# Second weight matrix: maxima on ScalarE, scaling and rounding in one pass, low half on VectorE, and new written orders

## The chip, the cores and the metric

The kernel runs on one core of one Trainium2 chip. The core has TensorE (PE; its weight loads are shown as PEld), VectorE (DVE), ScalarE (ACT), GpSimd (POOL) and the queue engine SyncE (SP), which issues the DMAs here. The metric is the device time of one execution in microseconds. Before the change it was 1485.22 us, the median of 3 runs (1484.78 to 1485.92).

## The reference

```python
def _attn_ref(q, k, v):                      # q, k, v: 8 x 8 x 1152 x 64, f32; q and k have a spread of 0.8
    q_pool = q.reshape(B, H, S // 2, 2, D).mean(axis=3)
    scores = scale * np.matmul(q_pool, k.transpose(0, 1, 3, 2))
    scores = scores - np.max(scores, axis=-1, keepdims=True)
    attn = np.exp(scores)
    attn = attn / (np.sum(attn, axis=-1, keepdims=True) + 1e-09)
    return np.matmul(attn, v).astype(np.float32)

def _moe_ref(x, w_in, w_out):                # x: 4608 x 512; w_in: 512 x 2048; w_out: 2048 x 512, both float64
    h = x @ w_in
    g = h * np.cos(h)
    return (g @ w_out).astype(np.float32)
```

The attention's output, heads side by side, is `x` of the second part.

## The kernel before

**Numbers.** An f32 product is made of f16 products: each operand is split into a rounded f16 half ("hi") and what the rounding left, again f16 ("lo"), and three matmuls (hi·hi, hi·lo, lo·hi) are summed in PSUM.

**Attention.** Heads are worked on in 32 pairs. For a pair, PE first forms scores for their row maxima (L645, L667, L690, L724, L794), and VectorE reduces them (L657, L678, L703, L739, L809). Then PE forms the scores again, transposed and with the maxima taken off (L1089, L1109, L1131), ScalarE takes the exponential out of PSUM (L1160), rounds it to f16 (L1168), GpSimd (or VectorE, L1170) makes the low half (L1174), and PE multiplies with the values (L1212, L1275; in the first six pairs part of the exponentials stay in f32). Four PSUM banks, the `st` ones, serve the maxima and the scores in turn; two, `ava` and `avb`, collect the outputs; two, `f`, serve the feed-forward part.

**Feed-forward.** For each of 18 chunks of 256 rows PE forms `h` (`ffn1`, L1509), ScalarE and VectorE bring it out (L1536 to L1540) and make the cosine (L1443, L1449), ScalarE rounds the product (L1460), GpSimd makes its low half (L1461), and PE multiplies with the second weight matrix (`ffn2`, L1572). These matmuls lie between those of the attention from 178 us on, and alone after its last ones.

**Weights.** `w_in` and `w_out` are float64 and come as eight blocks each of 128 x 1024 numbers. A block is decoded to f32 by three VectorE passes over its bits (L392, L395, L398; two of them work in place). Then its greatest magnitude is found (`weight_decode`): for `w_in`, where `WACT` is 1, by a ScalarE pass that squares the block and accumulates (L405, the squares go to a part of the weight tile that is written later), for `w_out`, where it is 0, by a VectorE reduction (L409). For each two blocks PE spreads the maxima over the partitions (L339) and VectorE makes a power of two of them (`weight_scale`). Then `weight_split` scales the block in place on ScalarE (L432), rounds it to f16 on ScalarE (L433) and makes the low half by four GpSimd subtractions of 256 columns each (L436). The blocks of `w_out` are held in buffers `wf`, which are of the same four large ones (`big`) that the feed-forward part uses.

**Order.** The instructions of each engine run in an order that is written out in the table `ORDER`, one packed string for each engine; `unpacked` turns it into a list of places, `arrange` chains the instructions in it. Matmuls are taken in lots of up to 12. The lists of PE (2684 lots), ScalarE (1632), VectorE (2104), GpSimd (783) and SyncE (492) fix every engine's order; a semaphore wait makes all behind it wait.

Of the kernel before, what the change touches and what calls it, by code (L numbers as in the profile page):

```python
# [74 lines left out]
ORDER = {  # L75
    "PE": (
        "c-l=?Yi|@s5UlQ**}a#|88|Q(I53<oe8l$odBMRkU>;Efk%Ex&As>=2NRjgYzo)8a?PPqu$4+lQs;hbyz|M|uYnhwDF+=<CX"
        "5l+br&B!WR@&t9bgx@!QkUIz!^Vb>V;R=l)C`T@+JYv-P#PK}SaQqBEEVUk4D@nl#H2Sk|4lD`Lb-TJaGJTBE~R8cT4n9gAf"
# [3 lines left out]
        "4rO^0H=1E^rKtpIoF17_DpA9T1jM)%XC7b{76dL@G-NF6mT1_hkHfLEM}9k1Z+xw9nBU{~X)c6s0&D@>m}3_QQ8$yL?R=NKW"
        "AoB3#HvLbEtg*z_zY~YJrO1~^GB?4TG+376hVgz%7IqN({o;W;eja0H~No3v*OK`tM`3weJ23Y4!5Rq@rW?0&+`QibmLLRsY"
        "eEM$qUORaa=!=Q`Q~e#F`WKEkQkxQUvx>_!I0M%QUMu3p;?F7>=~7F0rY2LEB}O;4<=STH+4Lmoc~8Cjp;576knAc#prAR`!"
        "`B?@&rdI6OmC?H$?&L685b<}n5;0QN}#GEzbhO@U|3XrbTf#UcF6a00Awp&XHGaff!6grnQg(d!9Bt!=twojdZko6e}263lc"
        "QI^~ygTCVV;EPuk4K!`r)SF~yA?G$!Sc`M1HJUyaazE9CxftYd#lF?qj=769qCKI=Jiu?hM5b<YW2wb@sgTVmT>;8=GO~+Cn"
# [5 lines left out]
        "PGEcU0oRguC)HmY-bp|RjwzjUOPAJls(&-nSc{$z822R=EIwRHrOf2gaS`V3oxU#&Z<><dgu*Mt^n7gH;eZfFoZawkVrX$X9"
        "jT&p{L<+8>O#1@kJf%Le8lIkv0Kk4uCJ-s@AA|C^G1&NRiLoyFSWHA>uSm`!s}DPr!S)TR~i3-zwoVC{u}>DPa((d@#0%d$)"
        "Xbs0fOevZ;Jidr3e2Q5_=b?GcjPj_DT~ss#^KWkUX92ONefZdMp!Ok0%?kWH{6*bgMS7U!{FrhH9Kp0(@iuA7YZC1!}Yzipu"
        "r5MwIAQ8jb1`652re+SQE#@Gm>~Ni6"
    ),
    "Activation": (
        "c-mc5?QUa53_bREKJG_KZ<E|6O`5dn(smJxRtWYFAVHr1i8p`;;P--f0K`l0@l1*kqvXzvXKWwa$D<H||DzxXBv|4Uf+W>s5"
        ";VmQSymzuCT5Zh8Y7TXqO3&eQckj4AoXy0N+t8K>&7vSL+OV{jQs!}<T4Be=*Dg^vwrM3F8VKqL7`oTPD;mP;)oWKa2BP@;O"
# [12 lines left out]
        "c-lo(%W@l45Iub#bMKvzW+Yj%WLuUcMRqJpwqtAoNgys>DOf;QP({ds@F-Y?;uBbf${(;~n?GPl6_sL}U*H3%{DSH3kwcfQk"
        "?!Mk_vzC;FqS}&zxpE}WRwMRk-r)v%jjg8MUY(!I0v60cZfvj@lwaymJOE8u(=+uZOBneay`V@LC7=TWV|S7ylTjMVg#fZno"
        "TsaEM)<{y}#d1F~xDy`*yq2E(+wli=y8LrG$?6zLD-#WqG$;F4LmN)<}^f4I5$JDa)z~gR;qp9|E};Qo3Vfj1?{dTlP^f9~c"
        "lxa-1Ybv7*`r$DBWfKpC%k&QdM&E_W_)(40w#p{h*5DRCxFxX585=M1Wl)fO_-D2l?HiVxUa!YFbyo14hs#h8HQ68;22`#kU"
# [1734 lines left out]
```

## Time and profile before

| what | us |
|---|---|
| median of 3 runs | 1485.22 |
| the profiled execution, its own time | 1485.77 |
| its span | 1484.0 |
| PE busy in the span | 1454.9 (98%) |
| ScalarE, VectorE, GpSimd busy | 1173.0, 1057.2, 915.8 |
| mean granted clock of PE | 0.996 |

All times in the rows further down are those of the profiled execution and count from the start of its span. An engine's busy time is the union of its instructions; PE's matmuls overlap, so a matmul's own duration is longer than the step from one to the next. The time after `<-` in brackets is how long the engine sat idle before the instruction, with what ended it.

### The profile page before, as it was taken

How to read it: one execution, taken by the hardware profiler on the slowest of the kernel's cores; microseconds unless marked ns; L12 is line 12 of the kernel's file. 1: busy time of each engine (PE TensorE's matmuls, PEld its weight loads, DVE VectorE, ACT ScalarE, POOL GpSimd, SP SyncE). 2: the span in 40 equal slices, each digit the busy share in tenths (PEclk: the TensorE clock that was granted, in tenths of full speed). 3: DMA queues.
4: the chain of work that ended last, by engine and by line, in shares of the span. 5: the costliest groups of instructions: out<-in, count | busy, mean ns of one | idle time of the engine just before them, and what ended most of it. 6: DMA issues, size and time to landing. Idle time of an engine off the chain costs nothing.

```text
span 1484.0 us, 36198 instructions
## 1 busy us (share of the span) xinstructions
PE 1454.9 (98%) x14825; PEld 979.1 (66%) x14825; DVE 1057.2 (71%) x2104; ACT 1173.0 (79%) x1728; POOL 915.8 (62%) x786
## 2 busy tenths in 40 slices
PE   6999999999999999999999999999999999999998
PEld 3777776657666666657666657666666657666665
DVE  7899886767787778867767867886778868443332
ACT  4667879988899788888979888989889888854442
POOL 4334658787677767586666576667867774723222
PEclk9999999999999999999999999999999999999999
DMA  8876742445445544456444654554445543200000
GB/s 247 219 218 167 200 112 56 112 110 104 111 91 108 115 102 104 104 120 142 99 105 79 120 112 106 96 130 104 97 102 106 122 110 69 48 20 22 29 11 29
DMA packets 280422, 158.07 MB, mean 107 GB/s; under 512 B 254784, under 2 KB 257088, under 8 KB 278208
## 3 DMA queue, kind: packets, MB, share of 16 engines
q1 hardware_dynamic: 280256, 155.76, 45.5%
q8 instruction: 116, 1.90, 0.5%
q14 instruction: 50, 0.41, 0.1%
HBM read 74.45 MB, written 10.49 MB: 57 GB/s over the span
## 4 chain that ended last, share of the span: by engine, by line
PE 89%; DVE 5%; ACT 4%; issue 1%; POOL 0%; DMA 0%; ACTq 0%; POOLq 0%; DVEq 0%
PE f L1509 21%; PE f L1572 20%; PE st L1089 15%; PE ava L1212 9%; PE avb L1212 7%; PE mx L645 4%; PE st L1572 3%; PE st L1509 2%; PE st L1109 2%; PE ava L1275 1%; ACT e L1160 1%; PE avb L1275 1%; DVE mxs L657 1%; ACT pp L1168 1%; PE mx L667 1%
## 5 line engine op out<-in xcount | busy, mean ns | idle before, releaser
L1174 POOL TENSOR_TENSOR pp<-e,pp 128x512 f16<-128x512 f32 (+1 forms) x464 | 519.3, 1144 | 256.2 <-ACT pp L1168 142.1
L1509 PEld LDWEIGHTS <-w 128*128 128x128 f16 x3456 | 329.2, 98 | 69.4 <-issue 13.1
L1509 PE MATMUL f<-xT,w 128*128 128x256 f16 x3048 | 367.1, 273 | 0.8 <-DVE y L1540 0.8
L657 DVE TENSOR_REDUCE mxs<-mx 128x1 f32<-128x512 f32 x464 | 295.0, 682 | 59.7 <-PE mx L645 59.4
L1572 PE MATMUL f<-w,g 128*128 128x512 f16 x1440 | 332.9, 379 | 0.0
L1160 ACT ACTIVATE e<-st 128x512 f32<-128x512 f32 x482 | 268.2, 598 | 78.6 <-PE st L1089 54.6
L1168 ACT CAST pp<-e 128x1024 f16<-128x1024 f32 x267 | 281.2, 1062 | 12.6 <-PE avb L1212 8.0
L1572 PEld LDWEIGHTS <-g 128*128 128x128 f16 x1680 | 157.4, 98 | 179.0 <-issue 7.6
L1212 PEld LDWEIGHTS <-pp 128*128 128x128 f16 (+1 forms) x4621 | 220.0, 98 | 78.9 <-issue 11.6
L1461 POOL TENSOR_TENSOR g<-hsc,g 128x512 f16<-128x512 f32 x144 | 179.1, 1260 | 141.6 <-ACT g L1460 134.2
L1089 PE MATMUL st<-q1T,k 128*128 128x512 f16 x576 | 219.1, 380 | 7.7 <-DVE mxs L739 3.2
L1089 PE MATMUL st<-q2T,k 128*128 128x512 f16 x576 | 219.4, 381 | 0.0
L1212 PE MATMUL ava<-vc,pp 128*128 128x65 f16 (+4 forms) x2800 | 165.8, 205 | 0.6 <-DVE pp L1170 0.6
L1540 DVE SCALAR_TENSOR_TENSOR y<-f,r1a,y 128x512 f32<-128x512 f32 x127 | 94.7, 747 | 95.3 <-ACT y L1539 95.0
L1212 PE MATMUL avb<-vc,pp 128*128 128x65 f16 (+3 forms) x2329 | 156.6, 207 | 1.4 <-POOL pp L1174 1.2
L1089 PEld LDWEIGHTS <-k 128*128 128x128 f16 x1152 | 99.5, 99 | 75.9 <-issue 16.7
L1449 DVE TENSOR_TENSOR hsc<-hsc,y 128x512 f32<-128x512 f32 x144 | 112.8, 811 | 43.4 <-ACT y L1443 43.4
L563 POOL TENSOR_TENSOR kst<-kld,kst 128x1152 f16<-128x1152 f32 x30 | 74.2, 2472 | 66.9 <-ACT kst L562 66.1
L1536 DVE TENSOR_SCALAR hsc<-f,small 128x512 f32<-128x512 f32 x111 | 82.6, 745 | 26.4 <-PE f L1509 26.2
L1460 ACT CAST g<-hsc 128x512 f16<-128x512 f32 x144 | 85.0, 620 | 18.4 <-DVE hsc L1449 14.5
L1539 ACT ACTIVATE y<-f,r1a 128x512 int32<-128x512 f32 x127 | 87.7, 691 | 13.8 <-DVE hsc L1536 13.1
L1160 ACT ACTIVATE pp<-st 128x512 f32<-128x512 f32 (+1 forms) x108 | 59.5, 593 | 40.1 <-PE st L1089 28.1
(183 smaller groups left out, 1812.6 us busy)
## 6 DMA issues: line engine op xcount, KB each, us to landing
vld<-in_v_dram SPq DMA_DIRECT2D x32, 576.0 KB, 4.4
kld<-in_k_dram SPq DMA_DIRECT2D x30, 576.0 KB, 4.9
qld<-in_q_dram SPq DMA_DIRECT2D x30, 576.0 KB, 4.3
k<-k SPq DMA_DIRECT2D x64, 144.0 KB, 3.1
wraw<-in_moe_w_in_dram SPq DMA_DIRECT2D x8, 1024.0 KB, 8.0
wraw<-in_moe_w_out_dram SPq DMA_DIRECT2D x8, 1024.0 KB, 6.4
out_dram<-ob SPq DMA_DIRECT2D x32, 256.0 KB, 2.7
...
```

The source lines that it names most:

```text
L657: nc.vector.reduce_max(mxs[n][:, h * QT + t, c : c + 1], banks[2 * c + h], axis=AX.X)
L1089: nc.tensor.matmul(s[y].rearrange("p (t c) -> p t c", c=P), kcol(w, j, h), x[:, h * QT : (h + 1) * QT, :], start=part == 0, stop=part == 1 ...
L1160: nc.scalar.activation(e[:, c], b[:, 0 : c.stop - c.start], AF.Exp, scale=exp_scale, bias=bias)
L1168: nc.scalar.copy(pp[:, 0, c0:n], e[:, c0:n])
L1174: nc.gpsimd.tensor_sub(pp[:, 1, c], e[:, c], pp[:, 0, c])
L1212: mm = nc.tensor.matmul(out, w, x, start=start, stop=False, skip_group_check=True)
L1449: nc.vector.tensor_mul(hj, hj, y[:, j : j + 2])
L1461: nc.gpsimd.tensor_sub(gt[:, 1], hj, gt[:, 0])
L1509: mm = nc.tensor.matmul(ps[:, fi, :], w1[wt][:, hp, fs], ck.xT[hp][:, xi, cs], start=n == 0, stop=n == 3 * HP - 1, skip_group_check=True,)
L1539: nc.scalar.activation(yj.bitcast(I32), ps, AF.Copy, scale=ra, bias=0.25)
L1540: nc.vector.scalar_tensor_tensor(yj, ps, ra, yj.bitcast(I32), ALU.mult, ALU.subtract)
L1572: nc.tensor.matmul(po, gt[:, gi, f % 2, ts_], w2[wt][:, f, :], start=f == 0 and (gi, wt) == (0, 0), stop=f == NF - 1 and (gi, wt) == (1, 0),)
```

## The change

`WACT` becomes 1 for `w_out` too: the VectorE reduction (L409, 8 of them) is replaced by a ScalarE square with accumulation, and the power of two is made from the square. With `WFUSE` 1 for `w_out`, ScalarE writes the f16 half straight from the unscaled f32 block with the scale as an operand (one pass in the place of L432 and L433), and VectorE makes the low half as block times scale minus high half (one pass over 1024 columns in the place of four GpSimd subtractions). `w_in` keeps its steps. All five lists are replaced.

```diff
-WACT = (1, 0)
+WACT=(1,1)
 HB = 2 * WACT[0]
...
+WFUSE = (0,1)
...
 ORDER = {
     "PE": (
...
@@ weight_split
         fv = ft.rearrange("p (r w) -> p r w", r=rows)
+        if WFUSE[wi]:
+            nc.scalar.activation(hi, fv, AF.Copy, scale=sc)
+            nc.vector.scalar_tensor_tensor(lo, fv, sc, hi, ALU.mult, ALU.subtract)
+            return
         nc.scalar.activation(ft, ft, AF.Copy, scale=sc)
         nc.scalar.copy(hi, fv)
         for o in range(0, rows, rows // WCUT):
```

Unpacked, the new lists hold 2684, 1632, 2104, 751 and 492 places: on PE and SyncE the same work, on ScalarE and VectorE as many instructions as before, on GpSimd 32 fewer. Few neighbours stay neighbours: 549 of PE's 2684 lots keep the lot that followed them. On PE no lot is moved by more than 53 places, on SyncE no DMA by more than 25. Three stretches of the two lists of PE and VectorE, by line of the kernel before (`x4` is a lot of four matmuls; `pair` is a lot of two L1089; head pairs are counted from 0):

```
A  VectorE, maxima of head pair 2 (before: from 57 us)
   before  L739  L392  L395  L739  L398  L739  L761  L739
   new     L739  L761  L739  (small)  L392  L739  ...
           (the reduction that follows L392 and L395 before now follows L761)
B  PE, scores of head pair 6's remaining rows (before: from 233.7 us)
   before  L1109 x12  pair  pair  L645 x4  pair  pair  L1509 x12
   new     L1109 x12  pair  L1212 x4  L1212 x4  L1212 x4  pair  L1509 x12  L645 x4
           L1509 x12  pair  pair
C  PE, maxima of head pair 5 (before: from 167.7 us)
   before  L645 x4  L1212 x12  L1212 x6  L1212 x4  pair  pair
   new     L645 x4  pair  pair  pair  L1212 x12
   VectorE at the same place
   before  L959  L1334  L1339  L1342  L657  L657  L657  L657
   new     L1339  (new low half)  L1342  L657  L657  L959  L959  L392  L657  L657
```

In the new lists the first L1509 of PE stands at place 361 (350 before) and the first L1572 at 528 (534 before). ScalarE's last two passes for `w_out` stand at places 236 and 239 (before the last four at 236 to 250), VectorE's last two low halves at 378 and 382; in the lists of before, these places are at 223 to 228 us of the profiled execution. All eight new low halves stand at VectorE places 256 to 382, where the list of before runs from 152 to 227 us.

## Rows read from the trace of the kernel before

**Rows 1.** The page's part 1: busy us, share of the span, instructions of each engine.
```profile
PE 1454.9 (98%) x14825; PEld 979.1 (66%) x14825; DVE 1057.2 (71%) x2104; ACT 1173.0 (79%) x1728; POOL 915.8 (62%) x786
```

**Rows 2.** Busy time by stretch: start:end, length, engines with instruction counts, granted clock, DMA.
```profile
0.00:37.00 37.00, 24.64 (x167) 13.11 (x167) 27.27 (x54) 16.52 (x26) 15.02 (x18) 0.95 0.84 248
37.00:100.00 63.00, 60.08 (x537) 47.02 (x536) 55.46 (x97) 43.62 (x73) 25.35 (x22) 0.95 0.78 216
100.00:150.00 50.00, 47.38 (x469) 36.49 (x468) 47.92 (x99) 36.58 (x62) 19.12 (x17) 1.00 0.63 176
150.00:200.00 50.00, 49.94 (x509) 38.48 (x508) 42.11 (x92) 40.33 (x67) 33.20 (x40) 1.00 0.68 177
200.00:245.00 45.00, 41.78 (x412) 30.98 (x409) 35.24 (x74) 40.80 (x61) 31.47 (x35) 1.00 0.35 85
...
300.00:700.00 400.00, 396.50 (x4278) 257.77 (x4276) 302.13 (x610) 344.52 (x503) 287.13 (x238) 1.00 0.50 110
700.00:1100.00 400.00, 399.97 (x4345) 263.93 (x4343) 303.93 (x607) 346.98 (x497) 275.75 (x228) 1.00 0.47 104
```

**Rows 3.** The same view for the two stretches with PE's clock lowered.
```profile
28.40:31.80 3.40, 3.17 (x8) 0.87 (x7) 3.28 (x6) 1.18 (x3) 0.00 (x0) 0.50 0.98 361
...
62.40:69.20 6.80, 6.80 (x25) 4.90 (x25) 3.24 (x4) 1.20 (x2) 4.08 (x4) 0.51 1.10 329
```

**Rows 4.** Timeline, 57 to 63 us: start, length, instruction, idle time before it.
```profile
57.76 2.21 DVE L392 TENSOR_SCALAR w<-wraw 128x1024 uint32<-128x1024 uint32 x1
...
60.01 1.72 DVE L395 SCALAR_TENSOR_TENSOR w<-wraw,w 128x1024 uint32<-128x1024 uint32 x1
...
61.65 0.68 DVE L739 TENSOR_REDUCE mxs<-m 128x1 f32<-128x512 f32 x1
...
62.38 0.45 PE L1089 MATMUL st<-q1T,k 128*128 128x512 f16 x1 [1.79 <-DVE mxs L739]
```

**Rows 5.** Timeline, 233.5 to 242 us.
```profile
236.71 1.53 ACT L1160 ACTIVATE e<-st,nb 128x512 f32<-128x512 f32 x3 [0.20 <-DVE nb L1190]
...
237.45 0.38 PE L1089 MATMUL st<-q1T,k 128*128 128x512 f16 x1 [2.03 <-ACT e L1160]
...
241.19 1.03 PE L1509 MATMUL f<-xT,w 128*128 128x256 f16 x8 [0.82 <-DVE y L1540]
```

**Rows 6.** Timeline of PE, four places between 104 and 684 us.
```profile
104.95 0.68 PE L690 MATMUL mx<-k,q1T 128*64 128x512 f16 x6 [0.60 <-DVE mxs L657]
...
537.32 0.38 PE L1089 MATMUL st<-q1T,k 128*128 128x512 f16 x1 [0.40 <-DVE mxs L657]
...
591.68 0.29 PE L1212 MATMUL ava<-vc,pp 128*128 128x65 f16 x4 [0.61 <-DVE pp L1170]
...
683.29 0.29 PE L1212 MATMUL avb<-vc,pp 128*128 128x65 f16 x4 [0.83 <-POOL pp L1174]
```

**Rows 7.** Instructions of the weight tiles: count, duration min/median/max in ns, first and last start.
```profile
L436 POOL TENSOR_TENSOR w<-wf,w x32: 666/672/904, 153.1 to 238.8; 128x256 f16<-128x256 f32 x32
...
L398 DVE SCALAR_TENSOR_TENSOR wf<-wraw,wf x8: 1216/1218/2182, 99.0 to 199.3; 128x1024 uint32<-128x1024 uint32 x8
L409 DVE TENSOR_REDUCE wmx<-wf x8: 1207/1216/1222, 127.3 to 203.2; 128x1 bf16<-128x1024 f32 x8
L432 ACT ACTIVATE wf<-wf,wsc x8: 1132/1152/1192, 149.8 to 229.6; 128x1024 f32<-128x1024 f32 x8
L433 ACT CAST w<-wf x8: 1028/1044/1059, 151.9 to 235.0; 128x1024 f16<-128x1024 f32 x8
...
L405 ACT ACTIVATE w<-w x8: 1042/1058/1060, 45.4 to 124.0; 128x1024 f16<-128x1024 f32 x8
L405 ACT ACTIVATION_READ_ACCUMULATOR w<-w x8: 189/200/208, 46.3 to 125.0; 128x1 bf16 x8
```

**Rows 8.** The first readers of the weights, in the same view.
```profile
L1509 PE MATMUL f<-xT,w x3048: 269/273/283, 178.2 to 1448.4; 128*128 128x256 f16 x191
L1572 PE MATMUL f<-w,g x1440: 377/379/390, 272.0 to 1458.6; 128*128 128x512 f16 x180
```

More of the change, by code (lines that the diff above doesn't have):

```diff
@@ L82 @@
[L82 to L86, printed above, removed]
@@ L92 @@
[L92 to L95, printed above, removed]
+        "c-m!F*>Y1y5Ix<q-K))#0a;}N1_L&hZIEP3$QW-J3?xtmm8B{nmC8eshg9;I|Ig`}>+p~++0vam)9dNe17K?_dha$j<Na$<0"
+        "Y4$S(P-q>)^s==;#Lv4`Jd<w6RbAk1|loy^?E6Zs&uO8q?Wb=Y7qg2%R!ui+FPnoxte^t4TTfYO1+Bx1#aVRCy3rbJf9_sB*"
@@ new lines @@
+        "$HjB7AgJK;SdQQKfyUr+%JS?f4?<BA*@qo8$$4yFjhB5Uc35ywZG1Tdqjr678$G#oc_(gYd;t(w2luiqIziMB37-J2i?hWbx"
+        "i24Y8)n!FCO#@2G{#Vj1ZIRkV-i{^&zU(e*+Ioq$ej#k@B?cEW-)J#EHYQ8T<)2I-{v<=}%?A6?*X&~1BJq)I$m(R5%sD-&0"
+        ">z2gHz1d{2l?J$@-FgqFpi{qU-3xWzY#VE)M8GkfWETZ!<MPQ&wb5&Qmxx695%BEIMXK%O|>>0(W*l|5tim`7iT(EDy?#%!#"
+        "j$l>R4mz}6HF>msvCA!5_abgE5V87kz3OGv7D<&ub}jVdiUh3RD^6x_B)i`##R`&v7*}uu1mZB=Hs>~XP`R}xZ~o3M)!RW!5"
+        "gy^;*u3<6S>-mv-qEL;f_aAh0&6=+5YV2(U50@B`K;gEq)w(ocQk>HLAJU45Ia<u(Pc*;>I1<REf{#I>47hy3-0lV+enX+U@"
@@ new lines @@
+        "UOS%uF!P1@TR6Pgn+z$vmIP)@I60mVTMAg{!BiS`8djA4DG8N_z>Wgf5v28~d11g`Yc#mNm)@Q@S0|6mdM2iN(Wh)_sk-$C9"
+        "h;{dQBVZ4eL3B_?9lGlWzpg1N{6urOQJNpt59tV6hG7TmQI57};HBL4cSq(PYut_gN$Q!F6IB}O_m!{UVS`jW@VqGUh}JWtw"
+        "u7m9{)Y#L(6Ewb~H!8v90hh&ygzeXM7L$Ls+bP?H)QkcYyZa-n4gwhK%y5!bl7^1RA=jS8{hvASO<C4fBa4v(-ScJRUoiS*6"
+        "1Jh}CN+yF;4i{1G8_w@oK*txATv<oFbOzv;@0i8(I`_ycn!eEBqBVvtmrT)o{*2j=2bLsesUaXOx%B=v5=IP^ypY$rUFj(KR"
+        "zoTT;W851B?8NsIMOXuGL*ix7vpQSyA9cqdek6N%H^YP)gC>b9F(H4@!Kgw-m)~P1(`2MRsLq71~#4(ZKU{`*!7`MK*o%-6Q"
@@ new lines @@
+        "(P6=x3+OBtu#N`gaM?m@NOhe!Uf}Ck%kY+)k|JEyE*cN|XWC#PGf9tyoL|R#tNkyJ$QWLZsgp<O1oCrga1iqpZVkY#4h}>Kr"
+        "Kp;wU3;YL_WDICZf~n7YB}o^kGN_JYJPhCH^hIi4Cj?l(-i+c1QVnJMhmA8;*?k{VgCAFGtD7&FiHF#o2ZnGFjyY)+$f{ZY|"
+        ")a8w#Pz;?pw-_Ye@RhSTR6mTLL%l;&*n_Ae<3$m@h7nY2$v}t(gk9?h7ltbIXpD&7oMoH<+zAr3lOPnsrL<Idge@4Y~){Y52"
+        ";^vdwj%N+^QjvM+@w{)NmO!ZTNT>SAdw=3T67FZV@D_=%dTZ`{qnXfc-r*d0g)3?(11Gz))Ke;A^VX-RzWy?5ugL3gZ&D6U-"
+        ";lR(S%#M6M#HhaImOAP)rAN@%Z9l3SypjWG==CZgv>rqojXpYYBU@0`URahfBn8;sedd$y?V#@ALLth%`YYD-)!3bL4=6)xN"
@@ new lines @@
+        "m;^{-gUrrJ(O-tSk1#wCJg;Fa(SNmX`1J0z1r+It1WQZ>^9qh>)6e!^*jTs^=ib7iSHFrn6CSNs`rY19DC#$sn&{GMN?Plv*"
+        "hBX5K<vJ?Jdy3JrgQmwH7z4ed)>|p0rp-kxpH3uWF{??Izpp9S%iRUFj1Bei}rq+H4|qPTqNuj5^l7DiI(DL&||{JqxK4<$i"
+        "dxS~zdPn{Xut&PnWSQ+%h?j+jbP2dRzOIHB<&mD^CIZAXHKJ&%=q^6)tGp`);<(n|+X=3wHl#U{LW2O83&YV&`HFmX(OH_T{"
+        "2n^T6lM1Z{rQ_Mx%o0Bta#C4gM;czga;|AgY?E08)p#(>(PFrL_xSW;<<vx(%__46Vx3ebN$4M5@`ylAl;=PYU5h(T)Laa|~"
+        "_^mMk+yduYC;8GWyE}45D!aU7;7@Ht$a7nbIDvb{9)v$wiI7er$9M}J>~M#3I6HDUp>4ZkYMF|)tb(i(LCKAeE*X1ex+22Yy"
@@ new lines @@
+        "wPSDEl)34`<LZYcCBP6s_S(xH*9H_Gv{{=S<uQ&$n~S72f1RPm{w6#3A2j!p&NcT4s{&2BUX`IpfhJ>jYEgIYUvp_m5@^AT~"
+        "hVz)cMb1$*d_s#jGhNTZkZ?2=t64*#V-h#jV;Dn6pd~HrFzl3zaqyaiAqP1lYH*FiIF#4M|2k1ag`)cg|*%GEr&uaYIbmeQ="
+        "+*tiOxpY?svAsHvu?$YY^ER4IA0zuc(^L%-BTKxz^(CNCxaALI#Vf2p`GQrj)AvBq{AiUJPUpUw^0V~bz)ULG$!h1>Kk|A{Z"
+        "+Ud+FQKAu}%zepq~;pM$k;um{lgNt^D)A@G8>yIj5@O9~eZ$XIJ4-~8gV1cuTaP1=U?;@+XrWl@G7lAytl7?SD1agZ?(>pvp"
+        "QHwh~0FO^R_sHNP2kdVTkwAiKRmT&*5@s{?jn8jk=6f?P^2a}jlzwm9GO7GM@&A`Z&HTiM`L1u_>#M)B6TQ8$Y*`@Yt*6Chp"
@@ L110 @@
+        "X0&`MMSA}BXnrqKje*=L^LUiCzL^+$bg47;#eu2;iCiA7(N>b7L&G=R+pr;7<7uy>wigZBDn"
     ),
     "DVE": (
[L112 to L115, printed above, removed]
@@ new lines @@
+        "dE&T`{hGd5k<nYL|*Lo;?G!_av)tje+~O*w!rG#7LAD$!Lj;G-Iihk2!V<D61PWrZ4JWQR$WlxAQGm8-g`$3_K3FqCxzS6Hi"
+        "5meKK0CCay12;s>Mvr2*cFq#;y5xn<EymOBA7?T=VSpg7bSxR76YRE^2!e-VEtoBkGEZ-A*)i0D6xFFa-mN9~G^?Ko~rFZe9"
+        "wHeV7oH4?;69SQ@do%>b@=#V)g#r4gy-Qglj9~f4M;(Gku9PM$vKm!8uu2}Qs(Rq^EOYd5zKWI_70ry+Hdw2r6x6BmR)WDuf"
+        "ORvi_oPIu=9CK#D3m;#TCsHsGrpU|QvX20p!Vz6kTmeg7lzj(L+?hfh>%hTG2}re=q7Ke-oB7(;H=3-yx<>ErC+Z3YEA-p^S"
+        "<P%AY!z)b%zjh4VYL4*hu^%v*w?}>O^){5%MJ##|(_aWyH$9peTe4EtjfQ*N+}H*4izBJE34$uUCSc72q~FT;Z7XN0gVC0mq"
@@ new lines @@
+        ";W61aIpj%%7_#+ept#9A~Ru}Ei0rT+5swOWfe;1w3qN#rIWNG_gzho76B7Ug)6%4+p(SjxuLo74OEFSh?hf42<l9w;M~B|dI"
+        "YpIJd@p`}Z?a{=sJ1PHjiBycTF{~ULh+}q6{`s#WY7A79M!r)@SJDz>|;0es3xPQ;#3}E9P{PbBw|MFO=@AW-}%WHzruiz7Z"
+        "5))ifKl8agpy;92Cz5Z2u^EwdG#*SaK>M6EM=?nuZP&HXoHOc9$E+x!>UGeGPMjxv<k9`^A|t<QG1lr`B<00NoPgqKB)}9|O"
+        "8=msmR1HLI1Skg!Q3Hsq`Yt<tWOT4M{8EwK;|ApunB{SsxpDhI00I5NQh-&#m6);5>?fEQrK-5*J+-rPzpFQJye=nPvkR`E-"
+        ">GvjzftlX8teQdd<0U>?Urer&NkH3#_p0R+L{gP_u$AdZ&gFIAJDZt4zbtzo>82n>RM5zL624^>>;A6g@4XoIWmQoHeN=yH6"
@@ L141 @@
-        "YW$J4w|s^l}k`}qgfQv|g"
+        "c-l>oOLoOD3_=n5*iQPo|K&b#C(R%^juE;-01%l$G7f76kfB#FVoF!Di=b8YB$C7w16*(I2-YTw-1$KN8Wj~u$fqq%9;}pKN"
+        "t7ca)%MIispnRK>m^k;T?(WUg88fB$i+NZj4sqLGerk<(_gdZlE5ZOnMhkA*90`E{o7UUuF^nEOA5ION4{=`+tqlneq1(YYW"
+        "ck-f&^wvERn<^s&X2!(<G3g`YR(*uY%gK9`p%}!oaNyoI8CZJ{};k)u)ZB&>Yxqo9g&m9+{R(smoV8x`CdLLpdT4)^Vhs9Nt"
+        "hXiMuI3cVqbf1iqUC1d;"
     ),
```

58 lines of the change are left out of this document (15 added, 43 removed).

## The prediction, made before the run

> **What bounds the kernel now.** I read the page's engine times first: PE is busy for 1454.9 us of 1484.0, no other engine for more than 1173.0 [rows 1]. So at most 29.1 us of idle PE can be won, since the change takes no matmul away and adds none. Next, busy time by stretch [rows 2] shows where they lie: 12.4 us in the first 37, 2.9 from 37 to 100, 2.6 from 100 to 150, 0.1 from 150 to 200, 3.2 from 200 to 245, 3.5 from 300 to 700; from 700 to 1100 PE idles for 0.03 us of 400. Two thirds of the kernel have nothing to give. In the early stretches VectorE is the second bound: 55.5 of 63 us and 47.9 of 50; from 200 to 245 it is ScalarE, 40.8 of 45. The clock rows add something: PE runs at half clock from 28.4 to 31.8 us and from 62.4 to 69.2, and in the second PE is busy for all 6.8 us [rows 3], so 3.4 us of work at full clock took 6.8. Then I looked at single gaps in the timeline [rows 4 to 6].
>
> **The edits by themselves.** All stand beside PE.
> GpSimd: 32 subtractions of 0.67 us go [rows 7]. They end at 239.5 us and the first reader, L1572, starts at 272.0 [rows 8], so no matmul waits for them; directly this is worth 0.
> ScalarE: 8 x 1.152 (L432) and 8 x 1.044 (L433) go, 17.6 us; 8 squares come at 1.058 + 0.200 for the accumulator, 10.1 us (their twins for w_in), and 8 scaled passes of the same 1024 columns, bounded by 1.04 (the unscaled cast) and 1.19 (the longest L432), taken at 1.15 because they carry the scale: 9.2 us [rows 7]. Together +1.7 us on ScalarE, of 81.1 busy in the 95 us from 150 to 245 [rows 2].
> VectorE: 8 reductions of 1.216 go, 9.7 us. The new pass reads two blocks of 1024 columns; the nearest row is L398, 1.218 in the median and 2.18 at worst [rows 7]. I take 1.25, so 10.0 us; the bound above is 17.5. Together +0.3 us, at most +7.7. It matters where: the reductions lie at 127 to 204 us, the new passes at places that before ran at 152 to 227, out of the fullest stretch of VectorE and into one where it was busy 77.4 us of 95.
> Cover for all this is the slack of the readers. w_out ends before at 239.5 us; the last new low half stands at VectorE's place of 226 us, and even 8 passes at the worst price put it near 234, against 272. Freeing `wf` earlier gives no matmul an earlier start, since PE is full from 245 on.
> The Trainium skill speaks against one of these moves: "ScalarE: Activation LUTs", Rules for kernel authors, says that a max belongs on VectorE and not on ScalarE (its figure for the gain is for bf16). The rows give 1.216 us for the reduction and 1.258 for the square, a draw in f32; by the rule ScalarE would lose, by the rows it loses 0.04 us per block, 0.3 in all, off the path either way.
>
> **The orders.** So the time is made by the new lists. I go through the gaps that the trace names.
> (a) 62.4 us. VectorE runs L392 (2.21 us) and L395 (1.72), decoding a weight block, before the reduction that frees a bank for PE; PE idles 1.79 us, and half clock follows at once [rows 3, 4]. In the new list neither of the two is ahead of this reduction (stretch A of the change). The gap should go, -1.8. The half clock that followed cost 3.4 us; whether it goes too I can't read off, because the lists differ in what precedes it: I count half, -1.7.
> (b) 237.5 and 241.2 us. Two pairs of scores follow the remaining rows of pair 6 directly, and the second pair's bank is freed only by the exponential that waits for the row bias; PE idles 2.03 us, and 0.82 soon after [rows 5]. The new list puts 12 small matmuls and then runs of 12 L1509 between (stretch B); a run of 12 is over 1.3 us by its neighbours' pace (8 of them span 1.03). I take 2.4 of the 2.85.
> (c) Single gaps of 0.60, 0.40, 0.61 and 0.83 us, 2.4 together, behind VectorE three times and behind GpSimd once [rows 6]. A new list has gaps of its own of this size, so I take half, -1.2.
> (d) The first 37 us, where 12.4 us are idle and the list is quite different: no sign can be read, 0, between -3 and +3.
> (e) A new gap: at stretch C the maxima of pair 5 are followed at once by three pairs of scores, where before 22 small matmuls lay between, and on VectorE a new low half (1.25 us) stands just ahead of the reductions that free the banks. The nearest row is (b)'s: +1.5, between 0.6 and 2.5.
> (f) SyncE issues the same 492 DMAs in another order, none moved by more than 25 places. No gap of (a) to (c) was ended by a DMA, so 0; a late transfer of q or k would show as in (d).
> Sum: -1.8 - 1.7 - 2.4 - 1.2 + 0 + 1.5 = -5.6 us. From the profiled execution's 1485.8 this is 1480.2; that execution is 0.55 us above the median of the runs, so 1479.6 on the scale of the median, which I predict.
>
> **Rivals.**
> The gaps only move. A list is fixed before the run, but durations are not: the same L398 takes 1.22 us or 2.18 [rows 7]. The new list then has as many misses as the old one, in other places: the 5.6 are lost but for (a)'s 1.8, which makes 1485.2 - 1.8 = 1483.4; with (d) at its upper end 1486. For it: the gaps at (c) are of several kinds, none systematic. Against it: (a) and (b) are plain in the list itself, and are mended there.
> More is gained. All idle PE from 37 to 700 us, 12.3 us, goes, and the half clock's 3.4: 1485.2 - 15.7 = 1469.5. For it: the same list order works without idling for 400 us. Against it: VectorE is 96% busy from 100 to 150 us, which no order mends.
> Slower: the added VectorE pass is a plug. It can't be cut as the four subtractions on GpSimd could; each time that it stands ahead of a reduction whose bank PE wants, PE waits for its length. If all eight do so at 1.25 to 2.18 us, that is 10 to 17 us, and with (a) to (c) won, -7.1, the time is 1488 to 1495; 1490 as a point. It decides where PE has less other work than one pass within reach, which up to 178 us is the case (no L1509 before 178.2 [rows 8]); from there on the feed-forward matmuls fill in. Stretch C is one such place for certain.
> That the edits don't do what they say would show as instructions: I see no way to it in the diff.
>
> **How the numbers follow.** Forecast, 1475 to 1483: 0.55. More gained, below 1475: 0.12. Gaps only move, 1483 to 1488: 0.19. Slower, above 1488: 0.14. What a measurement of this kernel can tell from no change is 0.2%, 3 us, so faster means below 1482.3 and slower above 1488.2: of the forecast's 0.55 some 0.5 lies below 1482.3, which with 0.12 makes 0.62 faster; 0.14 slower; 0.24 the same. The range that leaves out 2 in 10 takes in half of either end: 1470 to 1490. The forecast's own is 1475 to 1483.
>
> **What would show it.** Right: PE's idle time falls from 29.1 to some 24 us, no wait of a L1089 over 1 us near 60 and 235 us, one stretch of half clock instead of two, the same 700 to 1100 stretch. The edits: 8 more squares and accumulator reads on ScalarE, 1.15 us for its scaled pass, 1.25 for the new VectorE pass, 20 us less on GpSimd. Wrong: PE waiting for VectorE right behind a new pass between 150 and 230 us, a first L1572 that waits for w_out, or a start (first 37 us) with clearly more than 12.4 us idle.

## The result, and the profile after

The changed kernel took 1472.3 us, the median of 4 runs (1469.9 to 1474.7); before took 1485.6 beside it (1484.8 to 1487.2, 4 runs). The ratio is 0.9909, 95% interval 0.9891 to 0.9928: 13.3 us faster, where 5.6 were forecast. Two more series of the same kernel gave 0.9911 (0.9897 to 0.9925) and 0.9914 (0.9901 to 0.9928). The profiled execution took 1472.4 us, its span is 1470.3.

Part 1 of the page of after (busy us, share of the span, instructions), which answers to [rows 1]:
```profile
PE 1448.0 (98%) x14825; PEld 979.1 (67%) x14825; DVE 1048.8 (71%) x2104; ACT 1172.1 (80%) x1736; POOL 887.9 (60%) x754
```
PE has the same 14825 matmuls and is busy 6.9 us less; its idle time went from 29.1 to 22.3 us, 6.8 less. The two together are the 13.7 us by which the two profiled executions differ. Line numbers of after are up to five higher than those of before: L392 is L393 there, L657 is L662, L1089 is L1094, L1160 is L1165. Its new passes for `w_out` are L406 (square), L434 (scaled pass) and L435 (low half).

To see where it was made I cut both executions at equal work: the matmuls are added up along PE, each at the time that its shape takes in an unbroken run (0.216 us for 512 columns), and a stretch of after ends where its sum reaches that of before. By the times of before (us; differences of the two profiled executions; the end is that of PE's last matmul, some 4 us before that of the span):

| stretch of before | 0 to 37 | to 71.7 | to 134.1 | to 234.1 | to 250 | to 480 | to 714.6 | to the end | all |
|---|---|---|---|---|---|---|---|---|---|
| before took | 37.0 | 34.7 | 62.4 | 100.0 | 15.9 | 230.1 | 234.5 | 765.2 | |
| after took | 36.0 | 28.8 | 58.8 | 105.6 | 11.9 | 231.1 | 229.6 | 764.4 | |
| difference | -1.0 | -5.9 | -3.6 | +5.4 | -4.0 | +1.0 | -4.9 | -0.8 | -13.7 |
| forecast | 0 | -3.5 | -0.3 | +1.5 | -2.4 | 0 | -0.9 | 0 | -5.6 |

Two of these stretches in the view of busy time (start:end and length; busy time of PE, PEld, VectorE, ScalarE and GpSimd with instruction counts; granted clock, DMA share, GB/s), first of before, then of after, at equal work:
```profile
71.70:134.10 62.40, 60.02 (x570) 46.58 (x569) 60.32 (x109) 43.00 (x72) 24.71 (x21) 1.00 0.70 203
...
480.20:714.60 234.40, 231.11 (x2545) 151.17 (x2544) 180.64 (x372) 200.61 (x292) 166.13 (x136) 1.00 0.50 114
```
```profile
64.80:123.60 58.80, 58.73 (x584) 45.91 (x582) 51.79 (x99) 44.64 (x76) 23.48 (x22) 1.00 0.91 215
123.60:165.20 41.60, 38.40 (x364) 28.00 (x363) 39.51 (x75) 35.35 (x63) 18.99 (x22) 0.96 0.75 194
...
472.20:701.80 229.60, 228.66 (x2545) 150.54 (x2544) 179.09 (x371) 200.94 (x294) 160.38 (x134) 1.00 0.55 116
```
In the first, PE's idle time fell from 2.38 us to 0.07 and VectorE's load from 60.3 us of 62.4 to 51.8 of 58.8: weight passes on VectorE were put off (the decode passes alone took 29.6 us there before and 20.9 after). They come back in the next stretch, where VectorE is busy for 39.5 of 41.6 us and PE idles for 3.2. In the last, PE idles 2.35 us less, but the stretch is 4.8 us shorter, since PE is also busy for 2.45 us less with the same work. The trace says where most of that lies: a matmul of 512 columns ahead of a gap counts as busy for its 0.38 us, while in an unbroken run the next starts 0.22 after it, so each gap hides 0.16 us more; the stretch has 13 gaps of any length before and 2 after, which makes 1.8 of the 2.45.

Place (a), timeline of after (start, length, instruction, idle time before it), which answers to [rows 4]:
```profile
57.78 0.69 DVE L766 TENSOR_REDUCE mxs<-mx 128x4 f32<-128x512 f32 x1 [1.70 <-PE mx L756]
58.12 0.38 PE L1094 MATMUL st<-q1T,k 128*128 128x512 f16 x1
...
58.39 0.68 DVE L744 TENSOR_REDUCE mxs<-m 128x1 f32<-128x512 f32 x1
...
59.05 0.68 DVE L393 TENSOR_SCALAR w<-wraw 128x1024 uint32<-128x1024 uint32 x1
```
No decode pass stands ahead of the reductions; the next decode, L393, comes behind them, and PE has no wait here. The half clock of [rows 3] at 62.4 us is gone whole. (Half clock is a granted clock of 0.50 to 0.51 here, the lower of PE's two levels, 1.2 of 2.4 GHz.)

Place (b), which answers to [rows 5]:
```profile
228.35 1.00 PE L1217 MATMUL ava<-vc,pp 128*128 128x65 f32 x8
...
229.19 1.20 PE L1217 MATMUL avb<-vc,pp 128*128 128x65 f16 x12
...
230.66 0.38 PE L1094 MATMUL st<-q1T,k 128*128 128x512 f16 x1 [0.27 <-ACT e L1165]
```
2.2 us of value matmuls now stand where 2.03 us of idle time were; 0.27 us of idle time are left.

Stretch C, where after loses:
```profile
155.14 1.27 DVE L435 SCALAR_TENSOR_TENSOR w<-wf,wsc,w 128x1024 f16<-128x1024 f32 x1
...
157.32 1.56 POOL L581 TENSOR_TENSOR qld<-qld 128x576 f32<-128x576 f32 x1 [3.28 <-DMA qld<-in_q_dram]
...
157.63 2.33 DVE L435 SCALAR_TENSOR_TENSOR w<-wf,wsc,w 128x1024 f16<-128x1024 f32 x1
...
160.22 1.27 DVE L662 TENSOR_REDUCE mxs<-mx 128x1 f32<-128x512 f32 x2
...
160.95 0.59 PE L1094 MATMUL st<-q1T,k 128*128 128x512 f16 x1 [2.25 <-DVE mxs L662]
```
and the busy time around it:
```profile
155.00:160.20 5.20, 3.21 (x46) 1.64 (x43) 5.20 (x7) 5.20 (x11) 1.56 (x1) 1.00 0.61 130
160.20:163.70 3.50, 2.75 (x12) 0.76 (x13) 3.50 (x8) 1.92 (x6) 0.91 (x1) 0.51 0.78 248
```
The new low half stands ahead of the two reductions, and beside GpSimd's pass it takes 2.33 us and not 1.27. PE waits 2.25 us, and then runs at half clock for 3.4. VectorE and ScalarE are both busy for the whole 5.2 us ahead of the two reductions.

The edits, as durations (min/median/max in ns, first and last start), which answers to [rows 7] and [rows 8]:
```profile
L406 ACT ACTIVATE w<-wf x8: 1040/1060/1078, 138.8 to 210.4; 128x1024 f16<-128x1024 f32 x8
...
L434 ACT ACTIVATE w<-wf,wsc x8: 1132/1149/1158, 153.5 to 221.3; 128x1024 f16<-128x1024 f32 x8
L435 DVE SCALAR_TENSOR_TENSOR w<-wf,wsc,w x8: 1268/1282/2335, 155.1 to 223.2; 128x1024 f16<-128x1024 f32 x8
```

### The profile page after: what moved, and what is told of

It reads as the page before. It is cut to its first block, busy times and chain, and to the rows that moved or that the text cites. A ratio compares the mean times of both kernels' runs of the same rounds, so it can differ in the third digit from the quotient of the medians.

```text
span 1470.3 us, 36197 instructions
## 1 busy us (share of the span) xinstructions
PE 1448.0 (98%) x14825; PEld 979.1 (67%) x14825; DVE 1048.8 (71%) x2104; ACT 1172.1 (80%) x1736; POOL 887.9 (60%) x754
## 4 chain that ended last, share of the span: by engine, by line
PE 91%; ACT 4%; DVE 2%; issue 1%; DMA 1%; POOL 0%; SPq 0%; ACTq 0%; DVEq 0%
PE f L1514 21%; PE f L1577 21%; PE st L1094 16%; PE ava L1217 9%; PE avb L1217 6%; PE mx L650 4%; PE st L1577 3%; PE st L1514 2%; PE st L1114 2%; PE ava L1280 2%; PE avb L1280 1%; ACT e L1165 1%; PE mx L672 1%; ACT pp L1173 1%; PE avb L1577 1%
## 5 line engine op out<-in xcount | busy, mean ns | idle before, releaser
L1179 POOL TENSOR_TENSOR pp<-e,pp 128x512 f16<-128x512 f32 x464 | 521.3, 1148 | 293.9 <-ACT pp L1173 203.2
L662 DVE TENSOR_REDUCE mxs<-mx 128x1 f32<-128x512 f32 x464 | 295.1, 681 | 63.5 <-PE mx L650 63.1
L1165 ACT ACTIVATE e<-st 128x512 f32<-128x512 f32 x482 | 267.8, 597 | 80.8 <-PE st L1094 56.2
L1094 PE MATMUL st<-q1T,k 128*128 128x512 f16 x576 | 219.4, 381 | 2.6 <-DVE mxs L662 2.3
L1094 PE MATMUL st<-q2T,k 128*128 128x512 f16 x576 | 219.4, 381 | 0.0
L1094 PEld LDWEIGHTS <-k 128*128 128x128 f16 x1152 | 100.1, 99 | 73.6 <-issue 7.6
L1454 DVE TENSOR_TENSOR hsc<-hsc,y 128x512 f32<-128x512 f32 x144 | 108.5, 780 | 21.7 <-ACT y L1448 21.6
L1544 ACT ACTIVATE y<-f,r1a 128x512 int32<-128x512 f32 x127 | 87.5, 689 | 11.7 <-DVE hsc L1541 11.6
L1165 ACT ACTIVATE pp<-st 128x512 f32<-128x512 f32 (+1 forms) x108 | 59.2, 591 | 35.2 <-PE st L1094 31.0
```

Of the source, the lines that this page charges most:

```text
L662: nc.vector.reduce_max(mxs[n][:, h * QT + t, c : c + 1], banks[2 * c + h], axis=AX.X)
L1094: nc.tensor.matmul(s[y].rearrange("p (t c) -> p t c", c=P), kcol(w, j, h), x[:, h * QT : (h + 1) * QT, :], start=part == 0, stop=part == 1 ...
L1165: nc.scalar.activation(e[:, c], b[:, 0 : c.stop - c.start], AF.Exp, scale=exp_scale, bias=bias)
L1179: nc.gpsimd.tensor_sub(pp[:, 1, c], e[:, c], pp[:, 0, c])
L1454: nc.vector.tensor_mul(hj, hj, y[:, j : j + 2])
L1544: nc.scalar.activation(yj.bitcast(I32), ps, AF.Copy, scale=ra, bias=0.25)
```

## The experiments

Before lay at 1483.6 to 1485.1 us in these series, and after, on the same scale, at 1470 to 1472; each ratio is to before on the same chip. The diffs name instructions of the written lists, which the files hold packed.

**Edits and orders apart.** Theory: the new orders make the gain, and the edits are worth nothing by themselves. Rival: the edits make it.

e1_edits_alone, in the lists of before:
```
-  ScalarE  L432 scaled pass, L433 rounded pass     +  ScalarE  one fused pass at the place of L432
-  VectorE  L409 reduction                          +  ScalarE  L405 square, at the reduction's time
-  GpSimd   L436, four subtractions per block       +  VectorE  low half, behind its fused pass
```


> The three edits of the second weight matrix (maxima on ScalarE, one fused scaling and rounding pass, low half by VectorE) put into the written orders of before, every other instruction where it stood. Theory 1 (the gain of 13.3 us comes from the new orders, the edits price at nothing): within 3 us of before, so 1483 to 1489. Theory 2 (the edits make the gain, by 20.9 us less GpSimd work and 9.7 us less VectorE work): 1472 to 1475. Theory 3 (the added VectorE pass holds the score pipeline wherever it falls ahead of reductions): slower than before, 8 passes by 0.6 to 1.3 us each, 1490 to 1496.

1500.1 us, ratio 1.0107 (1.0093 to 1.0120): 16 us slower. Of the three theories only the third has the sign, and its time, 1490 to 1496, was still 4 us short. The timeline of e1 says how, and below it the busy time of the stretch that follows:
```profile
151.72 0.67 POOL L440 TENSOR_TENSOR w<-w,w 128x256 f16<-128x256 f32 x1
152.43 1.28 DVE L434 SCALAR_TENSOR_TENSOR w<-wf,wsc,w 128x1024 f16<-128x1024 f32 x1 [1.97 <-POOL w L440]
...
155.41 0.38 PE L1093 MATMUL st<-q1T,k 128*128 128x512 f16 x1 [2.07 <-DVE mxs L661]
```
```profile
156.20:169.90 13.70, 12.10 (x49) 8.96 (x48) 5.84 (x15) 8.23 (x15) 0.00 (x0) 0.50 0.21 59
```
The low half overwrites a buffer that GpSimd is still reading for `w_in`. VectorE stands 1.97 us for it, with the reductions of L661 behind; PE loses 2.07 us, and 13.7 us at half clock follow. A low half holds PE once more at 250 us, where it stands, with a pass of the feed-forward part, ahead of the reductions for the row bias; 6.8 us at half clock come with it (timeline and busy time):
```profile
244.62 1.50 DVE L434 SCALAR_TENSOR_TENSOR w<-wf,wsc,w 128x1024 f16<-128x1024 f32 x1
...
247.36 1.47 DVE L1191 TENSOR_REDUCE mq<-st 128x1 f32<-128x512 f32 x3
...
249.98 0.59 PE L1093 MATMUL st<-q1T,k 128*128 128x512 f16 x1 [3.80 <-ACT e L1164]
```
```profile
248.40:255.20 6.80, 5.16 (x16) 1.67 (x16) 3.94 (x10) 5.28 (x8) 2.45 (x3) 0.50 0.00 0
```
Before idles 2.03 us at this place (b), so 1.77 of the 3.80 are new.

e2_lists_alone, in the lists of after: the instructions of before at the same places, diff as above with the signs turned.

> The written orders of after with the instructions of before: two ScalarE passes where the fused one stands, the maxima on VectorE at the time of the squares, four GpSimd subtractions per block in place of the VectorE pass. Theory 1 (the orders make the gain): 1470 to 1476; it may even lie below after, since the VectorE pass of 2.3 us ahead of the late reductions at 160.2 us is gone (up to -5 us, 1467). Theory 2 (the edits make it): 1483 to 1487.

1485.8 us, ratio 1.0015 (1.0003 to 1.0026): theory 1 falls. The time lies in the range of theory 2, but e1 has shown that the edits alone don't make the gain either: it takes both. The orders alone gain nothing over the whole kernel, though up to 134 us they gain all that after gains there.

e7_fuse_undone and e8_maxima_undone, after with one edit taken back each:
```
e7  -  ScalarE fused pass, VectorE low half    +  ScalarE L437, L438; GpSimd L441 x4 at the low half's time
e8  -  ScalarE square                          +  VectorE reduction at the square's time
```


> After with only the fusion undone: two ScalarE passes and four GpSimd subtractions per block of w_out again, at the places of the fused pass and of the low half; maxima stay on ScalarE. e2_lists_alone (fusion and maxima both undone) lost 13 us between 165 and 245 us. Theory A (GpSimd's subtractions, 2.6 us per block ahead of the softmax low halves, and the second ScalarE pass did that): 1481 to 1487. Theory B (the maxima on VectorE did it): 1471 to 1474.

> After with only the maxima put back on VectorE, at the times of the squares; the fusion stays. Theory A (the fusion carries what the edits are worth in these orders): within 2 us of after, 1470.5 to 1474.5; the reductions at 158 us come ahead of the waiting ones as the low half does, so the gap at 160 us may grow by up to 2.4 us. Theory B (the maxima on ScalarE carry it): 1480 to 1487.

e7: 1484.7 us, ratio 1.0011 (1.0000 to 1.0022). e8: 1478.3 us, ratio 0.9967 (0.9955 to 0.9979). In the orders of after the fusion is worth 1.0%, some 15 us, as theory A of e7 had it, and the maxima on ScalarE 0.55%, some 8, which is between the two theories of e8. The two don't add up: undoing both, in e2, costs not measurably more than undoing the fusion alone. By stretches, as in the table above, one profiled execution each (that of e7 is 2 us below its median, that of e1 1.4):

| kernel | to 37 | to 71.7 | to 134.1 | to 234.1 | to 250 | to 480 | to 714.6 | rest |
|---|---|---|---|---|---|---|---|---|
| after | -1.0 | -5.9 | -3.6 | +5.4 | -4.0 | +1.0 | -4.9 | -0.8 |
| e2, orders without edits | -2.0 | -5.9 | -3.3 | +19.3 | -4.0 | +0.5 | -4.6 | -0.8 |
| e7, fusion undone | -1.4 | -5.9 | -3.6 | +16.6 | -4.0 | +0.9 | -5.1 | -0.8 |
| e8, maxima undone | -2.2 | -5.9 | -3.6 | +12.4 | -4.0 | +0.7 | -5.2 | -0.8 |
| e1, edits without orders | -1.2 | -0.3 | +0.6 | +11.6 | +2.4 | 0.0 | -0.3 | 0.0 |

Outside 134 to 234 us the four kernels with the new lists agree within 0.6 us from 37 us on, whatever the edits. So the gains there belong to the orders. Between 134 and 234 us, where `w_out` is scaled and split, the edits decide: with both the new lists lose 5.4 us, without them 19.3. The old instructions stand in these lists where I put them, at the places of the new ones; new lists made for the old instructions were not run, so this shows what the edits are worth in these orders, and not that no other order could do without them. What holds PE there (timelines) without the fusion, in e7 (line numbers differ by a few between the kernels):
```profile
229.41 2.86 POOL L441 TENSOR_TENSOR w<-wf,w 128x256 f16<-128x256 f32 x4 [0.96 <-ACT w L438]
232.23 1.15 POOL L1179 TENSOR_TENSOR pp<-e,pp 128x512 f16<-128x512 f32 x1
...
233.43 0.30 PE L1217 MATMUL avb<-vc,pp 128*128 128x65 f16 x4 [2.67 <-POOL pp L1179]
```
Four subtractions ahead of one softmax half. And without the maxima on ScalarE, in e8:
```profile
157.17 1.25 DVE L436 SCALAR_TENSOR_TENSOR w<-wf,wsc,w 128x1024 f16<-128x1024 f32 x1
...
158.34 2.34 DVE L411 TENSOR_REDUCE wmx<-wf 128x1 bf16<-128x1024 f32 x2
...
161.66 0.38 PE L1095 MATMUL st<-q1T,k 128*128 128x512 f16 x1 [3.42 <-DVE mxs L663]
```

**Place (a) by itself**, e4_reduce_first, the VectorE list of before:
```
-  L392  L395  L739  L398      (the reduction L739 that PE waits for at 62.4 us)
+  L739  L392  L395  L398
```


> Before, with one VectorE instruction moved: the reduction that TensorE waits for at 62.4 us goes ahead of the two decode passes (2.21 and 1.72 us) in front of it. Theory A (the gap of 1.79 us and the whole half-clock stretch of 6.8 us behind it, 3.4 us, hang on this order): 1480 to 1481.5. Theory A' (only the gap goes, the clock falls all the same): 1483.4 to 1484. Theory B (the idle time moves to the next wait, as the late decode then holds the weight tiles): 1485 to 1486.5.

1481.3 us, ratio 0.9980 (0.9972 to 0.9989), inside the range of theory A. The stretch to 71.7 us is 4.1 shorter with this one move: the gap of 1.79 us and the half clock both went. The decode passes now stand ahead of the next reduction, and a gap of 1.03 us is left there, with no half clock behind it (timeline):
```profile
60.63 1.58 DVE L398 SCALAR_TENSOR_TENSOR w<-wraw,w 128x1024 uint32<-128x1024 uint32 x1
...
62.86 0.38 PE L724 MATMUL m<-k,q1T 128*128 128x512 f16 x1 [1.03 <-DVE mxs L739]
```
By the medians the whole kernel gained 2.6 us, by the two profiled executions 4.5 (1485.8 and 1481.3). Before's 23 executions in this series reach from 1480.3 to 1486.5 us, with a mean granted clock from 0.999 to 0.996, so some of them seem to have less half clock than the profiled one; no trace shows such a one. In e4's profiled execution half clock came at another place (timeline, then busy time):
```profile
232.55 0.38 PE L1089 MATMUL st<-q1T,k 128*128 128x512 f16 x1 [2.03 <-ACT e L1160]
```
```profile
231.00:234.80 3.80, 2.12 (x8) 0.63 (x8) 1.97 (x6) 3.59 (x8) 3.57 (x6) 0.99 0.00 0
234.80:238.20 3.40, 3.00 (x13) 1.60 (x12) 2.67 (x10) 2.74 (x6) 3.26 (x4) 0.50 0.00 0
```
Just ahead of it lies the gap of (b), 2.03 us as in before, after which PE had kept its full clock in before (1.00 from 200 to 245 us [rows 2]).

**Place (b) by itself**, e10_a_and_b and e12_b_three_lists, both with e4's move:
```
PE (both)      -  L1212 x21 ahead of the remaining rows' scores    +  L1212 x21 behind them
ScalarE (e12)  -  L924  L433  L1160 x4                             +  L1160 x4  L924  L433
```


> Before with two local moves and no edit: the reduction ahead of the decode passes at 62 us (e4_reduce_first), and on TensorE five lots of value matmuls (21 of them, some 1.5 us) from ahead of the remaining rows' scores to behind them, where TensorE waits 2.03 us at 237.5 us. Theory A (each gap costs its idle time and the half clock behind it, and local moves take both away): the gap at 237.5 us falls to 0.3 to 0.8 us, no half clock there, 4 to 8 us below before, 1476 to 1480. Theory B (the moved matmuls only uncover other waits, as in e3): as e4_reduce_first, 1480 to 1482.

> As e10_a_and_b, and on ScalarE the bf16 copy of pair 6's values, which waits for the moved value matmuls, and the old rounding pass behind it (1.17 and 1.03 us) go behind the four exponentials that TensorE waits for. Theory A (e10's gap of 3.35 us was ScalarE standing on that copy): the gap falls to 0.5 to 1.2 us, no half clock, 3 to 4 us below e10_a_and_b, 1478.5 to 1480.5, ratio to before 0.996 to 0.998. Theory B (the chain scores, row maxima on VectorE, bias, exponentials holds it whatever ScalarE does first): the gap stays above 2 us.

e10: 1483.0 us, ratio 0.9996 (0.9986 to 1.0006), above the ranges of both theories; the gap grew (timeline):
```profile
231.67 1.16 ACT L924 ACTIVATE vc<-vld 128x1152 bf16<-128x1152 f32 x1 [2.65 <-PE avb L1212]
232.83 1.03 ACT L433 CAST w<-wf 128x1024 f16<-128x1024 f32 x1
...
234.98 0.59 PE L1089 MATMUL st<-q1T,k 128*128 128x512 f16 x1 [3.35 <-ACT e L1160]
```
ScalarE stands at L924 until the moved matmuls have read the old values, with the old rounding pass and the exponentials behind. e12: 1484.8 us, ratio 1.0005 (0.9996 to 1.0013). The first gap fell to 0.90 us as its theory A has it, but the time did not (0.996 to 0.998 was forecast): the two passes then held the next pair:
```profile
234.09 1.05 ACT L433 CAST w<-wf 128x1024 f16<-128x1024 f32 x1
...
235.68 0.37 PE L645 MATMUL mx<-k,q1T 64*128 64x512 f16 x1 [2.18 <-ACT e L1160]
```
So 2.2 us of ScalarE stood in the way at both places. L433, 1.03 of them, is one of the passes that the change takes away, but that is not what removes (b) in after: e2 and e7 keep it and gain the same 4.0 us in this stretch. Which of the further moves of the new lists do it was not isolated.

**Stretch C.** Theory: the low half ahead of the reductions makes the loss. Rival: VectorE is full here, and another pass takes its place. The moves, on the lists of after:
```
VectorE, after   L435  L662 x2  L964 x2  L393  L662 x2  L396  L708  L399
e3               L662 x2  L435  L964 x2  L393  L662 x2  L396  ...
e5               e3, and ScalarE's two L406 from 158 us behind the exponentials
e6               only ScalarE's move of e5
e9               L662 x2  L964 x2  L662 x2  L435  L393  L396  L708  L399, ScalarE as e5
e11, e13         e9, and L393, L396, L399 behind the small reductions; in e13 L399 later still
```


> After, with one VectorE instruction moved: the low half of the second block of w_out (2.33 us at 157.6 us) goes behind the two reductions that TensorE waits for at 160.95 us. Theory A (this pass in front of the reductions makes the gap of 2.25 us, and the half clock of 3.4 us that follows it is its consequence): the gap falls below 0.8 us, the half clock at 160 us goes, 1466 to 1468.5. Theory B (the wait only moves: the banks are late from the matmul side or the next VectorE pass takes the same place): 1471 to 1473.

> After, with the VectorE low half of the second block behind the two late reductions (as in e3_pass_behind) and the two ScalarE squares of the second pair behind the exponentials of the waiting scores (from 158 us to about 161.5 and 165 us). Theory A (both engines were plugged here, one pass each; with one alone moved the other still held TensorE): the gap at 160.9 us falls below 0.5 us, no half clock at 160 us, 4 to 5 us below after: 1466 to 1468.5, ratio to before 0.987 to 0.989. Theory B (a third wait takes their place, the matmul side or GpSimd's 384-column low half at 160.4 us): within 1.5 us of after.

> After, with only the two ScalarE squares moved behind the exponentials, the VectorE pass left where it was. Theory A (both plugs): the wait for VectorE's reductions stays, 1.5 to 2.3 us, and the half clock with it: within 1 us of after, ratio 0.990 to 0.9925. Theory A2 (the squares alone were the cause): 1466 to 1468.5, ratio 0.987 to 0.989.

> After, with stretch C put in the order in which TensorE waits for it: on VectorE all four late reductions and the two scaled values ahead of the second block's low half and of the next decode pass, on ScalarE the two squares behind the exponentials. Theory A (the gap at 160 us is VectorE's order and the half clock its consequence; e3, e5 and e6 each left one pass too early): no TensorE gap over 0.5 us between 155 and 170 us, no half clock there, 4 to 5 us below after's run of the same chip (ratio to before 0.987 to 0.989). Theory B (the passes have no room in this stretch: the displaced low half or decode pass holds the next consumer): within 1.5 us of after's run.

> After unchanged, so that e9_reduce_first_c has its comparison on the same chip: ratio to before 0.989 to 0.993; the gap at 160 us 1.2 to 2.3 us with a half clock of 3.4 us or more behind it. If theory A of e9 is right, e9 lies 4 us or more below it.

> As e9_reduce_first_c, and the three decode passes of the next w_out block (0.7, 1.2 and 1.2 us on VectorE at 161.4 to 165.1 us in e9) go behind the small reductions and the residual pass, where VectorE stood idle for 2.5 us. Theory A (VectorE has more work in this stretch than fits ahead of TensorE's waits; with 3.1 us less the gaps end): no TensorE gap over 0.8 us between 155 and 175 us, no half clock, 3 to 5 us below after's run of the same chip. Theory B (another engine holds TensorE there too): gaps of 1 us and more remain, within 1.5 us of after's run.

> After unchanged, the comparison of e11_decode_later on the same chip: ratio to before 0.989 to 0.993.

> As e11_decode_later, with the third decode pass (1.21 us at 170.0 us) moved on behind the maxima, the low half and the residual pass that follow. Theory A (an order without the loss exists, and the 5.2 us at C are order, not the amount of work): no TensorE gap over 0.8 us between 155 and 176 us, no half clock there, ratio to before 0.987 to 0.989, 3 to 5 us below after. Theory B (VectorE is short of time here, and the wait reappears behind the next pass): ratio 0.991 to 0.995.

| kernel | median us | ratio to before (95%) | longest wait of PE near C | 134 to 234 us against before |
|---|---|---|---|---|
| after_again | 1470.4 | 0.9911 (0.9897 to 0.9925) | 1.16, reductions on VectorE | +4.6 |
| after_third | 1471.4 | 0.9914 (0.9901 to 0.9928) | 2.25, the same | +6.2 |
| e3 | 1474.4 | 0.9935 (0.9922 to 0.9949) | 1.30, ScalarE | +6.6 |
| e5 | 1473.9 | 0.9942 (0.9924 to 0.9961) | 1.36, VectorE | +8.0 |
| e6 | 1472.7 | 0.9931 (0.9916 to 0.9946) | 1.16, VectorE | +5.7 |
| e9 | 1472.7 | 0.9924 (0.9911 to 0.9936) | 1.94, VectorE | +7.3 |
| e11 | 1475.9 | 0.9946 (0.9933 to 0.9958) | 2.33, VectorE, at 171.9 us | +10.3 |
| e13 | 1475.8 | 0.9941 (0.9926 to 0.9955) | 1.57, ScalarE, at 172.2 us | +10.7 |

The rival holds in kind: a wait comes up again each time. Not in size: only e13 lies in the range forecast for it; e3, e6 and e9 lie 0.8 to 1.4 us above theirs, e5 and e11 some 3, by the ratios. e6 and e9 can't be told from after. In e3 the next in line is ScalarE's square, in e9 a decode pass, in e11 the last of the decode passes (timelines; for e11 the busy time as well):
```profile
158.76 1.07 ACT L406 ACTIVATE w<-wf 128x1024 f16<-128x1024 f32 x1
...
160.88 0.38 PE L1094 MATMUL st<-q1T,k 128*128 128x512 f16 x1 [1.30 <-ACT e L1165]
```
```profile
162.15 1.23 DVE L396 SCALAR_TENSOR_TENSOR wf<-wraw,wf 128x1024 uint32<-128x1024 uint32 x1
...
164.03 0.38 PE L1094 MATMUL st<-q1T,k 128*128 128x512 f16 x1 [1.94 <-DVE mxs L708]
```
```profile
155.00:171.70 16.70, 12.08 (x123) 7.97 (x120) 16.03 (x25) 13.28 (x23) 8.08 (x6) 1.00 0.66 174
171.70:181.90 10.20, 10.02 (x51) 6.67 (x51) 9.23 (x14) 4.80 (x9) 0.00 (x0) 0.50 0.71 140
```
```profile
170.01 1.21 DVE L399 SCALAR_TENSOR_TENSOR wf<-wraw,wf 128x1024 uint32<-128x1024 uint32 x1
...
171.88 0.27 PE L340 MATMUL mx<-ident,mxa 128*128 128x128 bf16 x1 [2.33 <-DVE mxs L683]
```
e11 comes through C without a wait over 0.8 us, but VectorE is busy for 16.0 of 16.7 us on the way; the passes put off meet the next reductions, and 10.2 us at half clock follow. No move beat after, which stays the fastest kernel run. Whether an order exists that has these edits and no loss here is open: six kernels were not enough to say, and in e13 PE waits for ScalarE's copy of values, no longer for VectorE. After's own wait here was 1.16 us in one of its three profiled executions and 2.25 in two.

## Why the prediction was right or wrong

The sign held, and the wide range, 1470 to 1490, held the time; the size did not, 13.3 us against 5.6, and 1472.3 lies below the forecast's own range, 1475 to 1483, in a part that was given 0.12. The failing step is "So the time is made by the new lists", with the edits at 0 ahead of it: edits and orders were priced one by one and added. Alone, the edits cost 16 us and the orders 2; together they save 13. Within the sum the terms missed by -2.4 (a), -1.6 (b), -7.3 (c) and +3.9 us (e); that these cancel in part is luck. Of the signs named, PE's idle time fell to 22.3 us and the waits near 60 and 235 us went, as they should; but two stretches of half clock are still there and not one (27.1 to 30.5 us, and a new one at C), and PE waits right behind a new pass at 160.95 us, which was named as a sign of being wrong.

- **The edits, priced at 0 on the path.** The durations were right: 1.149 us for the scaled pass (1.15), 1.282 for the low half (1.25; at worst 2.34, bounded at 2.18), 27.9 us less on GpSimd, some 20 of it forecast for the 32 subtractions. What was wrong is the question. I asked which reader waits for `w_out`, and none does, in any kernel here. What the passes cost is what stands behind them on their engine: GpSimd's softmax halves in e2 and e7 (2.7 us at one place), the reductions in e8 (3.4), the exponentials in e10 and e12 (2.2 to 3.4). Before's own lists leave 0.1 us idle from 150 to 200 us [rows 2], and their one long wait behind it is (b); the new lists put the weight passes later, out of the stretch where VectorE was full, and into one where, as the old instructions were placed in e2, e7 and e8, only the edited ones left room for them.
- **The rule on maxima.** I called it a draw, off the path. In these orders the maxima on VectorE make the kernel 8 us slower (e8). The Trainium skill's rule ("ScalarE: Activation LUTs", Rules for kernel authors: max belongs on VectorE) goes by time per element and would have had them there; by the rows the two are a draw (1.216 us against 1.06 and 0.20), what decided in e8 was how full VectorE is at that place, and no run shows the rule's bf16 gain.
- **(a)** Right in place. -3.5 forecast, -5.9 measured. e4 shows 4.1 of it by the one move: the whole half clock went, where I counted half. Of the other 1.8, the gap of 1.03 us that e4 keeps and after has not is a part; the rest was not isolated.
- **(b)** Right in place, -2.4 against -4.0. e10 and e12 show that it was not the place of these matmuls alone: with them moved, two passes of ScalarE hold PE next. e2 and e7, which have the new lists and the old passes, gain the same 4.0.
- **(c)** Mis-sized, and the largest miss among the orders. I listed four gaps, 2.4 us, of the 5.7 that PE idles in the two stretches, and counted half of them. Between 71.7 and 134 us all of PE's idle time went, 2.3 us and not 0.3, and the stretch was 3.6 shorter; from 480 to 714.6 us idle time fell by 2.35 and the time by 4.9. So in these two stretches the time fell by 1.6 and 2.1 times the idle time that the view shows (3.6 over 2.3, 4.9 over 2.35). Of the difference, 0.16 us for each gap that went can be read off, as said above; the rest is not isolated, and that it is a cost of the gaps is not shown.
- **(e)** Right in place and mechanism, mis-sized: +1.5 against +5.4. The gap was 2.25 us, within the bound of 2.5, but I had not priced the half clock that follows such a gap, though [rows 3] had shown it for (a): 3.4 us at half clock are some 1.7 lost. The rest, some 1.5, was not isolated.
- **(d)** -1.0, within its bounds; three executions of after differ by 1.9 us in it.
- **The rival "slower"** named the right mechanism: e1 is that kernel, 1500 us, with the low half in front of the reductions at two places, each with half clock that the rival had not priced. One of them lies at 250 us, where the rival expected the feed-forward matmuls to fill in. That after isn't slower is due to its lists. "More gained" came nearest to the time (1469.5), yet not by its reason: 5.6 us of idle PE between 36 and 702 us and one half clock are still there.
